# Moving the short convolution's elementwise work to VectorE and pacing the convolution units by weights

## The chip, the cores and the metric

One core of a Trainium2 chip runs the kernel. The metric is device time in microseconds (us) of one execution; smaller is better. The engines are TensorE (PE, with its weight loads shown as PEld), VectorE (DVE), ScalarE (ACT), GpSimd (POOL) and SyncE, whose queue (SPq) issues most transfers.

## The reference, cut to what matters

Two branches read the same layer-normed tokens (2048 tokens, 512 channels) and are added to the input.

```python
# branch A: short convolution of k, product with v, long convolution, gate
for t in range(4):
    k_shift += k_pad[:, t:t + S, :] * shift_k[:, 3 - t]
kv = k_shift * v
y  = irfft(rfft(pad(kv)) * rfft(pad(ssm_k)))[:S] + kv * ssm_D
A  = xn * y
# branch B: 8 experts, 2 for each token, gates by softmax over the two logits
h   = silu(xn @ w1[e]) @ w2[e]            # w1: 512 x 1792, w2: 1792 x 512
out = x + A + sum over e of gate * h
```

## The kernel before, in words

The experts are the spine of the program. They run one after the other (`expert`, rank 0 to 7, by falling number of tokens). For each, the weights come in slices: seven of w1 (128x1024 elements) and eight of w2 (128x896), seven of 128x1024 for the last three experts. ScalarE rounds a slice to float32r (`wh`, line 844), VectorE subtracts to get the rest (`wl`, line 847), and TensorE multiplies with high and low parts (line 862). In the first half each 128 hidden rows go from PSUM through Silu on ScalarE (`ht`, line 886) and two VectorE operations (`h`, lines 889 and 890). The next expert's tokens are gathered by an indirect transfer on the POOL queue (line 787), transposed on TensorE (`ptx`, line 806) and split by ScalarE and VectorE (`xh`, `xl`, lines 809 and 810). At an expert's end its outputs are gated and added (line 912) and scattered.

After every slice the expert calls `fill`, so there are 15 calls for each of the first five experts and 14 for the next two. `fill` hands out the other branch's work piece by piece. The list `units` has, in this order: two K units (`conv_k`, the last quarter of the long filter), eight V units (`conv_v`: two halves of the channels by four groups of tokens), two empty places, the exchange of the buffer pool (`swap`), 32 group units (`group_unit`, the middle stage of the transforms), and two empty places. Each call adds `rate` to a counter; when it has reached 1, the next unit is started and every unit under way is moved on by one stage. The rate is set so that the list is used up near call 87, near the end of the sixth expert. After that the 16 `last_unit`s follow in the last two experts, at 1.4 for each call of a first half.

A V unit has three stages. The first loads k and v (and, at the head of each half of the channels, the short filter's weights `shr`, line 683, copied to `sb` on VectorE, line 685) and does eight elementwise operations: `kva = k*w3` (line 712), three times `kvb = k*wt` and `kva += kvb` (lines 714, 715), `kva *= v` (line 716). Two of the four token columns are done by VectorE and two by GpSimd, each in 128x512 operations. The second stage splits `kva` into `vp` (ScalarE line 604, VectorE line 606), the third multiplies on TensorE (lines 610, 611) and stores to `zv_d`. The tiles of a V unit share seven buffers (tag b4), k has two.

A group unit loads `z` from `zk_d` and `zv_d`, splits it (lines 587, 590), multiplies (nine 512-column matmuls in all), and works on the products with ScalarE and VectorE (line 745 is its first VectorE operation after the matmuls) before the result is stored to `zi_d`.

The order of the instructions on each engine is fixed at build time: a planner simulates the program and lays each engine's instructions down by program order and by when it believes their inputs and buffers to be ready. Each engine then works its list strictly in order.

Of the kernel before, what the change touches and what calls it, by code (L numbers as in the profile page):

```python
# [18 lines left out]
P = 128  # L19
S = 2048  # L20
D = 512
DC = D // P
DH = D // 2
# [19 lines left out]
WARM = 4  # L43
DELAY = 3.0
STEPS = 8
RND = 1.5 * 2.0 ** 23
# [15 lines left out]
def fft_constants():  # L62
    """Matrices of the two-stage transform of odd frequencies kappa = k1 + 256 k2 of length 8192.

    Tokens are n = 32 n1 + n2.  The filter comes with runs of 16 on the partitions (2 n1 + n2 / 16), the
    other operand with the float32r parts of its data on one half of the partitions each (high and low,
    or low and high), and the matrices of the 64-point stages come to match.
    """
    n1 = np.arange(N1)
    k1 = 2 * np.arange(N1) + 1  # L70
    ang = 2 * np.pi * np.outer(n1, k1) / 256.0
    fwd = np.empty((N1, N1, 2))
    fwd[:, :, 0] = np.cos(ang)
    fwd[:, :, 1] = -np.sin(ang)
    fh, fl = _split(fwd.reshape(N1, P))
    inv = np.empty((N1, 2, N1))
    inv[:, 0, :] = np.cos(ang.T) * (2.0 / 4096.0)
    inv[:, 1, :] = -np.sin(ang.T) * (2.0 / 4096.0)
    ih, il = _split(inv.reshape(P, N1))
    zf, zi = np.zeros_like(fl), np.zeros_like(il)  # L80
    first = np.zeros((N1, 2, 2, 2, P), np.float32)
    for h in range(2):
        first[:, h, 0, h], first[:, h, 1, h] = fh, fl
    edge = np.concatenate([first.reshape(P, 4 * P), np.concatenate([fh, fh]), np.concatenate([fl, zf]),
                           np.concatenate([zf, fl]), il, ih, il, zi, ih, zi], axis=1)

    n2 = np.arange(N2)
    k2 = np.arange(N2)
    mid = np.empty((G, P, 4, P), np.float32)
    for g in range(G):  # L90
        b = np.zeros((2, 2, N2, 2, 2, N2))
        for a in range(2):
            kk = k1[2 * g + a]
            th = 2 * np.pi * (n2[:, None] * kk / 8192.0 + n2[:, None] * k2[None, :] / 32.0)
            b[a, 0, :, 0, a, :] = np.cos(th)
            b[a, 1, :, 0, a, :] = np.sin(th)
            b[a, 0, :, 1, a, :] = -np.sin(th)
            b[a, 1, :, 1, a, :] = np.cos(th)
        b = b.reshape(P, P)
        mid[g, :, 0], mid[g, :, 1] = _split(b)  # L100
        mid[g, :, 2], mid[g, :, 3] = _split(b.T)
    mid = mid.reshape(G // 2, 2, P, 4 * P).transpose(0, 2, 1, 3)
    return np.ascontiguousarray(edge), np.ascontiguousarray(mid).reshape(G // 2, P, 8 * P)
# [5 lines left out]
def routing_constants():  # L109
    """Index tables for the routing, the same for any input."""  # L110
    p = np.arange(P)
# [31 lines left out]
class Builder:  # L143
# [13 lines left out]

    # ------------------------------------------------------------------ setup
    def setup(self):
# [23 lines left out]
    def after(self, late, early, reason):  # L183
        """Keeps the program order of two instructions (no semaphore)."""
        self.tc.add_manual_dep(
            late.ins, early.ins.name,
            mybir.DependencyInfo(mybir.DependencyClass.NoSync, mybir.DependencyReason.DATA), reason=reason)

    # ------------------------------------------------- layer norm and routing
    def load_x(self, ep, sp, cp):  # L190
# [32 lines left out]
    def logits(self, bp, sp, cp):  # L223
        """The gate's logits before the scaling by rstd, x @ (w - mean(w)), and layer norm's statistics."""
        nc, io = self.nc, self.io
# [75 lines left out]
    def norm(self):  # L301
        """Normalises tokens in place; the last of them release the stores."""
        nc = self.nc
# [19 lines left out]
    def floor_div(self, out, x, tmp, d, scale):  # L323
        """out = scale * floor(x / d) for integers 0 <= x < 4096, by rounding x / d - (d - 1) / 2d."""
        V = self.nc.vector
# [4 lines left out]
    def routing(self, bp, sp, cp):  # L330
# [160 lines left out]
        def pick(dst, mask, a):  # L491
            """dst = a where mask else dst (a is lost)"""
            V.tensor_sub(a, a, dst)
            V.tensor_mul(a, a, mask)
            V.tensor_add(dst, dst, a)
# [23 lines left out]
    def onehot(self, A, q, parts):  # L519
        """A[:, i, :] = onehot(q[:, i])"""  # L520
        n, width = A.shape[1:]
# [12 lines left out]
    def products(self, A, B, R, srcs, out):  # L534
        """out = onehot(row)^T @ [onehot(column) * v for v in srcs]"""
        nc = self.nc
# [15 lines left out]
    def slots(self, cp):  # L552
        """Token and gate of every slot, a few of the tokens' columns at a time."""
        V = self.nc.vector
# [24 lines left out]

    # ------------------------------------------------------------- long conv  # L580
    def split_pair(self, pool, tag, src, shape, hi_eng="act", bufs=None):
        """src (float32 AP) -> float32r parts hi, lo with hi + lo = src."""
        nc = self.nc
# [15 lines left out]
    def split_halves(self, pair, src):  # L599
        """float32r parts of src: of its rows 0..63 high over low, of its rows 64..127 low over high."""  # L600
        nc = self.nc
# [6 lines left out]
    def edge1(self, out, h, pair):  # L608
        """First stage of the transform of one half's tokens."""
        self.nc.tensor.matmul(out, self.ev[:, 0, :], pair[h], start=True, stop=False)  # L610
        self.nc.tensor.matmul(out, self.ev[:, 1 + h, :], pair[h], start=False, stop=True)

    def tokens(self, ap):
        """[S, d] rows as [half, n1, n2 in the half, d]"""
        return ap.rearrange("(n h j) d -> h n j d", h=2, j=NI)
# [13 lines left out]
    def load_k(self, cp, dc):  # L629
        """Long filter of 128 channels, the skip weight added to its first tap."""  # L630
        nc, io = self.nc, self.io
# [10 lines left out]
    def conv_k(self, cp, dc, c8, routed):  # L642
        """First stage of the long filter's transform, 128 channels and every other run of 8 tokens."""
        nc = self.nc
# [32 lines left out]
    def conv_v(self, cp, dh, c4):  # L677
        """kv = shift_conv(k) * v and the first stage of its transform."""
        nc, io = self.nc, self.io
# [25 lines left out]
        b = cp.tile([P, 4, DH], F32, tag="b4", name="kvb")  # L705
        for eng, i0, i1 in ((nc.vector, 0, 2), (nc.gpsimd, 2, 4)):
            r = slice(i0, i1)

            def w(t):
                return sb[:, t:t + 1, :].to_broadcast([P, i1 - i0, DH])  # L710

            eng.tensor_mul(a[:, r, :], k[:, i0:i1, :], w(3))
            for t in (2, 1, 0):
                eng.tensor_mul(b[:, r, :], k[:, i0 + 3 - t:i1 + 3 - t, :], w(t))  # L714
                eng.tensor_add(a[:, r, :], a[:, r, :], b[:, r, :])  # L715
            eng.tensor_mul(a[:, r, :], a[:, r, :], v[:, r, :])
        yield
# [39 lines left out]
    def last_unit(self, gp, i):  # L757
        """Last stage for tokens i of every run of 16; the products with the matrix's low part come apart."""
        nc, io = self.nc, self.io
# [18 lines left out]

    # ------------------------------------------------------------------- moe
    def gathers(self, r):  # L780
# [36 lines left out]
    def prep(self, r):  # L817
        """Rank 0's tokens come as they are and are normalised here, the others' come from xn."""
        nc = self.nc
# [45 lines left out]
    def expert(self, hp, r, fill):  # L865
        """The expert with the r-th largest number of tokens, on its first CAPS[r] slots."""
        nc, io = self.nc, self.io
# [112 lines left out]
    def overflow(self):  # L980
        """Tokens beyond an expert's static slots, in blocks of 96; as many blocks as the routing asks for."""
        nc, io, tc = self.nc, self.io, self.tc
# [40 lines left out]
    def build(self):  # L1023
# [14 lines left out]
        with ExitStack() as st:  # L1038
# [13 lines left out]
            slots = self.slots(cp)  # L1052
            units = [lambda c8=c8: self.conv_k(cp, 3, c8, True) for c8 in range(2)]
            units += [lambda dh=dh, c4=c4: self.conv_v(cp, dh, c4) for dh in range(2) for c4 in range(4)]
            units += [None, None, swap]
            units += [lambda g=g: self.group_unit(self.gp, g) for g in range(G)]
            units += [None, None]
            lasts = [lambda i=i: self.last_unit(self.gp, i) for i in range(NI)] + [None]
            live = []
            done = [-DELAY]  # L1060
            rate = (len(units) + DELAY) / (5.75 * 15)

# [11 lines left out]
            def fill(r, second):  # L1074
                next(slots, None)
                if units:
                    done[0] += rate
                    while done[0] >= 1.0:
                        done[0] -= 1.0
                        step(units)  # L1080
                elif not second:
# [33 lines left out]
```

## Time and profile before

| | |
|---|---|
| median of 3 runs | 1073.06 us (1069.16 to 1077.16) |
| profiled execution, span from first to last instruction | 1070.0 us |
| PE busy | 886.5 us (83%) |
| DVE busy | 697.2 us (65%) |
| ACT busy | 471.5 us (44%) |
| POOL busy | 365.2 us (34%) |

The profiled execution is given by its span alone. Busy times are sums over the whole span, and the stages differ much: the page's line of 40 slices (26.75 us each) has TensorE at 9 tenths in slices 15 to 29, but at 3 to 9 tenths in slices 7 to 14, which is where the V units run, and at 3 to 8 in the last ten, where the last units run.

### The profile page before, as it was taken

The numbers are of one execution on the slowest core, as the hardware profiler recorded it, in microseconds if no ns is written. First come the engines' busy times: TensorE is split into PE (matmuls) and PEld (weight loads), VectorE is DVE, ScalarE is ACT, GpSimd is POOL, SyncE is SP. The second block draws the span as 40 slices with busy tenths as digits, with TensorE's granted clock in tenths as the row PEclk, the third lists the DMA queues.
The fourth block names the chain that finished last, engine by engine and source line by source line (L and its number), as shares of the span: only waits on it lengthen the run. The fifth ranks groups of instructions, "written<-read, shape, count | busy, mean of one in ns | idle before, by whom it ended". The sixth has DMA issues, their size and how long they took to land.

```text
span 1070.0 us, 14726 instructions
## 1 busy us (share of the span) xinstructions
PE 886.5 (83%) x5440; PEld 793.4 (74%) x5440; DVE 697.2 (65%) x986; ACT 471.5 (44%) x705; POOL 365.2 (34%) x279
## 2 busy tenths in 40 slices
PE   9879993986678899999999999999956786452595
PEld 7669993985667799999999999888744564341484
DVE  7879736999898786687668865895544530442431
ACT  5663231344233466666665765675423320322220
POOL 1362046894778422041204140500222113231213
PEclk9879997997988999999999999999987898685798
DMA  7788477866665865666566666664744445424332
GB/s 269 242 280 280 165 153 183 232 184 144 167 163 146 269 190 176 201 201 190 176 201 203 200 169 199 201 202 128 226 107 117 95 100 122 121 62 117 90 99 83
DMA packets 175526, 183.27 MB, mean 171 GB/s; under 512 B 38150, under 2 KB 138880, under 8 KB 173980
## 3 DMA queue, kind: packets, MB, share of 16 engines
q1 hardware_dynamic: 132556, 143.03, 44.9%
q0 software_dynamic: 42896, 39.27, 15.1%
q8 instruction: 44, 0.72, 0.3%
q14 instruction: 30, 0.25, 0.1%
HBM read 140.09 MB, written 46.45 MB: 174 GB/s over the span
## 4 chain that ended last, share of the span: by engine, by line
PE 43%; DMA 27%; DVE 10%; issue 9%; POOL 2%; ACT 1%; SPq 1%; ACTq 0%; POOLq 0%; DVEq 0%
PE ps L862 33%; DMA out_dram<-xnb 12%; DMA xnb<-xn_d 5%; DMA shr<-in_A_shift_k_dram 3%; DMA acc<-out_dram,gix 3%; DMA out_dram<-acc,ids 2%; DVE wl L847 2%; DVE kvb L714 2%; DVE kva L715 1%; DVE vp L606 1%; DMA zv_d<-ev 1%; PE ptx L806 1%; DMA zb<-zi_d 1%; DVE h L889 1%; POOL out_dram L914 1%
## 5 line engine op out<-in xcount | busy, mean ns | idle before, releaser
L847 DVE TENSOR_TENSOR wl<-wraw,wh 128x1024 fp32r<-128x1024 f32 (+1 forms) x112 | 140.3, 1253 | 119.2 <-ACT wh L844 110.4
L862 PE MATMUL ps<-xh,wh 128*128 128x264 f32 (+6 forms) x728 | 189.6, 322 | 32.4 <-DVE acc L912 20.7
L844 ACT ACTIVATE wh<-wraw 128x1024 fp32r<-128x1024 f32 (+1 forms) x117 | 119.5, 1022 | 192.6 <-PE ps L862 95.7
L862 PE MATMUL ps<-h,wh 128*128 128x264 f32 (+3 forms) x1120 | 193.5, 291 | 0.0
L862 PE MATMUL ps<-xl,wh 128*128 128x264 f32 (+6 forms) x728 | 186.9, 318 | 0.0
L862 PE MATMUL ps<-xh,wl 128*128 128x264 f32 (+6 forms) x728 | 185.9, 317 | 0.0
L862 PEld LDWEIGHTS ps<-h,wh 128*128 128x128 f32 x1120 | 162.9, 191 | 2.2
L862 PEld LDWEIGHTS ps<-xh,wh 128*128 128x128 f32 x728 | 124.3, 194 | 45.0 <-ACT yb L774 20.5
L862 PEld LDWEIGHTS ps<-xl,wh 128*128 128x128 f32 x728 | 123.3, 193 | 7.4
L862 PEld LDWEIGHTS ps<-xh,wl 128*128 128x128 f32 x728 | 122.8, 193 | 7.9
L862 PE MATMUL ps<-h,wl 128*128 128x264 f32 (+3 forms) x560 | 119.4, 292 | 1.8 <-DVE wl L847 1.8
L886 ACT ACTIVATE ht<-ps 128x528 f32<-128x528 f32 (+6 forms) x112 | 68.0, 607 | 72.4 <-PE ps L862 34.4
L914 POOL DMA_INDIRECT out_dram<-acc,ids x42 | 59.6, 1419 | 113.3 <-DVE acc L912 104.0
L862 PEld LDWEIGHTS ps<-h,wl 128*128 128x128 f32 x560 | 90.4, 192 | 3.1 <-DVE wl L847 2.1
L890 DVE TENSOR_TENSOR h<-ht,h 128x528 fp32r<-128x528 f32 (+6 forms) x112 | 89.1, 798 | 2.1
L590 DVE TENSOR_TENSOR lo<-zb,hi 128x1024 fp32r<-128x1024 f32 x16 | 19.6, 1222 | 103.4 <-ACT hi L587 102.8
L899 POOL DMA_INDIRECT acc<-out_dram,gix x42 | 56.4, 1342 | 86.0 <-issue 38.9
L771 PE MATMUL psb<-hi,ei 128*128 128x512 f32 x32 | 13.3, 496 | 71.0 <-ACT hi L587 71.0
L787 POOL DMA_INDIRECT xg<-xn_d,gix x36 | 46.2, 1282 | 74.7 <-DVE tb L548 41.0
L933 PE MATMUL py<-wh,h 128*128 128x512 f32 (+2 forms) x168 | 68.4, 408 | 3.9 <-ACT wh L844 3.9
L776 POOL TENSOR_TENSOR xnb<-xnb,yb 128x512 f32<-128x512 f32 x16 | 22.7, 1422 | 140.7 <-DMA xnb<-xn_d 134.2
L934 PE MATMUL py<-wl,h 128*128 128x512 f32 (+2 forms) x168 | 68.5, 408 | 0.6 <-DVE wl L847 0.6
(257 smaller groups left out, 1601.3 us busy)
## 6 DMA issues: line engine op xcount, KB each, us to landing
wraw<-in_B_w_dram SPq DMA_DIRECT2D x77, 512.0 KB
wraw<-in_B_w_dram SPq DMA_DIRECT2D x40, 448.0 KB
zk_d<-ev SPq DMA_DIRECT2D x16, 512.0 KB
zv_d<-ev SPq DMA_DIRECT2D x16, 512.0 KB
z<-zk_d SPq DMA_DIRECT2D x32, 256.0 KB
mid<-in_c_mid_dram POOLq DMA_DIRECT2D x16, 512.0 KB
z<-zv_d SPq DMA_DIRECT2D x32, 256.0 KB
zi_d<-zo SPq DMA_DIRECT2D x32, 256.0 KB
```

The lines of the kernel that those rows point to most:

```text
L714: eng.tensor_mul(b[:, r, :], k[:, i0 + 3 - t:i1 + 3 - t, :], w(t))
L776: nc.gpsimd.tensor_mul(xn, xn, y)
L787: self.gather = nc.gpsimd.indirect_dma_start(out=t[:sb], out_offset=None, in_=self.xn_d[:, :] if r else self.io["A_q"].rearrange("o s d -> ...
L844: w = nc.scalar.activation(hi, raw, AF.Copy)
L847: t = (lo_eng or nc.vector).tensor_sub(lo, raw, hi)
L862: nc.tensor.matmul(ps[:, u, :n], w, x[:, u, :], start=first and w is wh and k == 0, stop=last and w is wl)
L886: acts.append(nc.scalar.activation(t, ps[:, :nu, :n], AF.Silu))
L890: self.hid = nc.vector.tensor_sub(l, t, h)
L899: nc.gpsimd.indirect_dma_start(out=acc[:sb], out_offset=None, in_=io["out"][:, :], in_offset=bass.IndirectOffsetOnAxis(ap=self.gix[:sb, c0 ...
L914: st = nc.gpsimd.indirect_dma_start(out=io["out"][:, :], out_offset=bass.IndirectOffsetOnAxis(ap=self.ids[:sb, c0 + b:c0 + b + 1], axis=0) ...
L933: nc.tensor.matmul(o, a, wh[:, f, :], start=ff == 0, stop=False)
L934: nc.tensor.matmul(o, a, wl[:, f, :], start=False, stop=False)
```

## The change

Comments and docstrings are removed. In `conv_v` the loop over two engines goes: VectorE does all four token columns in eight 128x1024 operations for each unit, and GpSimd does none. In `build` each unit has a cost (1 for K units, for the empty places behind the V units and for `swap`, 2.5 for V units, 1 for group units and the last two places); `rate` is formed from the sum of the costs, and `fill` starts a unit when the counter has reached that unit's cost.

```diff
+COST_K, COST_V, COST_G = 1.0, 2.5, 1.0
...
-        for eng, i0, i1 in ((nc.vector, 0, 2), (nc.gpsimd, 2, 4)):
-            r = slice(i0, i1)
-
-            def w(t):
-                return sb[:, t:t + 1, :].to_broadcast([P, i1 - i0, DH])
-
-            eng.tensor_mul(a[:, r, :], k[:, i0:i1, :], w(3))
-            for t in (2, 1, 0):
-                eng.tensor_mul(b[:, r, :], k[:, i0 + 3 - t:i1 + 3 - t, :], w(t))
-                eng.tensor_add(a[:, r, :], a[:, r, :], b[:, r, :])
-            eng.tensor_mul(a[:, r, :], a[:, r, :], v[:, r, :])
+
+        def w(t):
+            return sb[:, t:t + 1, :].to_broadcast([P, 4, DH])
+
+        nc.vector.tensor_mul(a, k[:, 0:4, :], w(3))
+        for t in (2, 1, 0):
+            nc.vector.tensor_mul(b, k[:, 3 - t:7 - t, :], w(t))
+            nc.vector.tensor_add(a, a, b)
+        nc.vector.tensor_mul(a, a, v)
...
-            units = [lambda c8=c8: self.conv_k(cp, 3, c8, True) for c8 in range(2)]
-            units += [lambda dh=dh, c4=c4: self.conv_v(cp, dh, c4) for dh in range(2) for c4 in range(4)]
-            units += [None, None, swap]
-            units += [lambda g=g: self.group_unit(self.gp, g) for g in range(G)]
-            units += [None, None]
+            units = [(COST_K, lambda c8=c8: self.conv_k(cp, 3, c8, True)) for c8 in range(2)]
+            units += [(COST_V, lambda dh=dh, c4=c4: self.conv_v(cp, dh, c4)) for dh in range(2) for c4 in range(4)]
+            units += [(COST_K, None), (COST_K, None), (COST_K, swap)]
+            units += [(COST_G, lambda g=g: self.group_unit(self.gp, g)) for g in range(G)]
+            units += [(COST_G, None), (COST_G, None)]
...
-            rate = (len(units) + DELAY) / (5.75 * 15)
+            rate = (sum(c for c, _ in units) + DELAY) / (5.75 * 15)
...
-                    while done[0] >= 1.0:
-                        done[0] -= 1.0
-                        step(units)
+                    while units and done[0] >= units[0][0]:
+                        cost, u = units.pop(0)
+                        done[0] -= cost
+                        step([u])
```

## Rows read from the trace of the kernel before

**Rows 1.** Windows: stretch, its length, busy us (and count) by engine, PEclk, DMA share, GB/s.
```profile
170.00:372.00 202.00, 147.81 (x1016) 140.34 (x1015) 182.80 (x166) 71.61 (x103) 149.40 (x99) 0.87 0.69 181
372.00:750.00 378.00, 377.26 (x2591) 352.13 (x2592) 280.67 (x392) 240.80 (x365) 85.40 (x74) 1.00 0.62 189
...
362.00:372.00 10.00, 5.74 (x47) 5.52 (x45) 3.60 (x5) 1.06 (x2) 8.17 (x8) 1.00 0.94 283
```

**Rows 2.** Whom TensorE waited for from 170 to 372: us in total, times, longest.
```profile
PE ps L610 <- DVE vp L606: 20.6, 4, 10.1
PE ptx L806 <- DVE xl L810: 20.5, 2, 16.5
```

**Rows 3.** The chain that ended last: start, us, piece.
```profile
150.12 18.39 DMA shr<-in_A_shift_k_dram
...
827.33 13.76 DMA out_dram<-xnb
```

**Rows 4.** VectorE by form from 168 to 362: count, busy us, mean ns, idle before.
```profile
L714 DVE TENSOR_TENSOR kvb<-k,sb 128x512 f32<-128x512 f32 x24 | 30.1, 1252 | 0.2
L715 DVE TENSOR_TENSOR kva<-kva,kvb 128x512 f32<-128x512 f32 x24 | 27.3, 1137 | 0.5
L606 DVE TENSOR_TENSOR vp<-kva,vp 64x1024 fp32r<-64x1024 f32 x16 | 26.2, 1640 | 1.3 <-ACT vp L604 0.8
L890 DVE TENSOR_TENSOR h<-ht,h 128x552 fp32r<-128x552 f32 x14 | 18.3, 1305 | 0.2
L847 DVE TENSOR_TENSOR wl<-wraw,wh 128x1024 fp32r<-128x1024 f32 x12 | 18.2, 1515 | 2.0 <-PE ps L862 1.6 <-ACT wh L844 0.3
L847 DVE TENSOR_TENSOR wl<-wraw,wh 128x896 fp32r<-128x896 f32 x9 | 15.0, 1672 | 0.1
...
L712 DVE TENSOR_TENSOR kva<-k,sb 128x512 f32<-128x512 f32 x8 | 12.5, 1558 | 4.0 <-DMA zv_d<-ev 4.0
L716 DVE TENSOR_TENSOR kva<-kva,v 128x512 f32<-128x512 f32 x8 | 8.4, 1044 | 0.2
L912 DVE SCALAR_TENSOR_TENSOR acc<-pty,gate,acc 96x512 f32<-96x512 f32 x6 | 4.1, 736 | 0.0
...
L810 DVE TENSOR_TENSOR xl<-ptx,xh 128x276 fp32r<-128x276 f32 x8 | 3.1, 434 | 0.0
```

**Rows 5.** The same view from 450 to 700, where no V unit runs.
```profile
L847 DVE TENSOR_TENSOR wl<-wraw,wh 128x1024 fp32r<-128x1024 f32 x19 | 23.2, 1222 | 12.6 <-ACT wh L844 10.9 <-issue 1.6
L890 DVE TENSOR_TENSOR h<-ht,h 128x528 fp32r<-128x528 f32 x28 | 19.7, 706 | 0.5
L847 DVE TENSOR_TENSOR wl<-wraw,wh 128x896 fp32r<-128x896 f32 x16 | 17.5, 1092 | 9.1 <-ACT wh L844 8.9
...
L889 DVE CAST h<-ht 128x528 fp32r<-128x528 f32 x28 | 12.2, 437 | 1.2 <-ACT ht L886 1.2
```

**Rows 6.** Tile kvb: ns min/median/max, first and last start.
```profile
L714 DVE TENSOR_TENSOR kvb<-k,sb x24: 675/1632/1789, 170.3 to 347.8; 128x512 f32<-128x512 f32 x24
L714 POOL TENSOR_TENSOR kvb<-k,sb x24: 1256/1628/2247, 171.4 to 340.5; 128x512 f32<-128x512 f32 x24
```

**Rows 7.** Timeline of VectorE: start, us, operation, idle before and what ended it.
```profile
168.53 1.09 DVE L685 COPY sb<-shr 128x1024 f32<-128x1024 f32 x1 [15.81 <-DMA shr<-in_A_shift_k_dram]
```

**Rows 8.** Timeline of TensorE inside expert 1, first and last of 26 rows.
```profile
206.76 0.41 PE L862 MATMUL ps<-xl,wh 128*128 128x276 f32 x2
...
213.14 0.42 PE L862 MATMUL ps<-xh,wl 128*128 128x276 f32 x2
```

**Rows 9.** The first window of Rows 1 again, line 862's matmuls and weight loads alone.
```profile
170.00:372.00 202.00, 124.06 (x868) 118.93 (x867) 0.87 0.69 181
```

**Rows 10.** Line 745 (one for each group unit): as Rows 6; then two of its starts.
```profile
L745 DVE TENSOR_TENSOR ka<-pu,ka x32: 683/692/693, 378.4 to 741.7; 128x512 f32<-128x512 f32 x32
...
454.03 0.69 DVE L745 TENSOR_TENSOR ka<-pu,ka 128x512 f32<-128x512 f32 x1
463.83 0.69 DVE L745 TENSOR_TENSOR ka<-pu,ka 128x512 f32<-128x512 f32 x1 [2.39 <-ACT ka L741]
```

## The prediction

> **What bounds the kernel now.** I read the windows first. From 372 to 750 us TensorE is busy 377 of 378 us at a granted clock of 1.00; from 170 to 372 it is busy 148 of 202 us at 0.87, while VectorE is busy 183 us there, its highest share of any long stretch [rows 1]. That is the stretch of the V units. Next, who is waited for: TensorE's two largest waits there, 41 us together, are both for VectorE, for `vp` and for the next expert's `xl` [rows 2]. So VectorE sets the pace from 170 to 372, and TensorE from then to about 750. Behind that, the chain that ended last runs mostly through the last units' accumulating stores, 14 us and more each, one after the other [rows 3]; they begin at fixed places of experts 6 and 7, so the tail starts earlier by whatever the front gains and keeps its length.
>
> Why is VectorE full? By form, every one of its operations that reads two SBUF tiles is slow between 168 and 362: `wl` 1515 and 1672 ns, `h` 1305 [rows 4], against 1222, 1092 and 706 ns where no V unit runs [rows 5]. The reader is to see in `kvb` that a 128x512 operation takes 675 ns at best and 1632 in the median, which is GpSimd's own median of 1628 [rows 6]: the two engines go in step.
>
> **How much TensorE loses.** Inside expert 1, 50 matmuls of 276 columns take 213.14 - 206.76 = 6.38 us, 0.1276 each [rows 8]. The 1016 matmuls from 170 to 372 [rows 1] are 868 of line 862 [rows 9], 64 of the V units (512 columns, by columns 0.237 each) and 84 transposes (128 columns at most, 0.06). At full pace that is 110.8 + 15.2 + 5 = 131 us, so 71 of the 202 us are lost, as idle time and as matmuls at half clock after a wait.
>
> **The elementwise work.** Removed: 64 GpSimd operations, 1.63 us each in the median. They leave only the stretch's slowdown with them. Added on VectorE: 8 units x 8 operations of 128x1024, which read two SBUF tiles as `wl` does: 64 x 1.222 [rows 5] = 78.2 us. Removed there: lines 712, 714, 715, 716, which sum to 78.3 us [rows 4]. So VectorE does GpSimd's half for nothing. The rest gets cheaper: `vp` 26.2 to 16 x 1.222 = 19.6, `h` 18.3 to 14 x 0.73 (706 ns by columns) = 10.3, `wl` 18.2 + 15.0 to 14.7 + 9.8; with the casts, some 30 us. Whether the repeated operand `sb` costs more in a longer operation no row shows; its 512-column form at 675 ns bounds two halves at 1.35, so between 0 and 32 x 0.13 = 4 us more; I take 0, from the nearest row.
>
> Here a rule is to be weighed. By rows 4 and 6 the half on GpSimd buys VectorE no time. The Trainium skill, Perfetto Trace Analysis, "Optimizing Scalar/DVE Operations", says that work of a saturated VectorE may be offloaded, even to GpSimd, though it adds that the two share an SBUF read port and that it might not help. By its first half the sum comes out slower, rival C; by its second, as mine.
>
> **The pacing.** Counting the calls of `fill` (rate 50/86.25 = 0.580 before, 62/86.25 = 0.719 after): K units start at calls 6 and 7, not 7 and 9; V units at 11, 14, 18, 21, 25, 28, 32, 35, not 11, 13, 14, 16, 18, 19, 21, 23; the last V matmuls at 38, not 26; groups from 41 to 84, not 30 to 83; the list ends at call 87 in both, and the last units keep their calls. So the V work is spread over 28 calls, not 16.
>
> What those 28 calls cost each engine. TensorE: 672 x 0.1276 / 15 = 5.72 us a call, 160, plus 15 for V and 5 for transposes: 180 us. VectorE, for each expert: 7 x 1.222 + 8 x 1.092 + 14 x (0.437 + 0.706) [rows 5] + 3.1 + 4.1 [rows 4] = 40.5 us, 2.7 a call, 76 in 28 calls; V adds 78.2 + 19.6 + 2 copies of `sb` (1.1 each): 176 us in all. The two are even, so VectorE's idle share decides. Bounds for its busy share: 0.905 (182.80 of 202) and 0.74 (280.67 of 378) [rows 1]. It is nearest to the first, a stretch with the same V chain: 176/0.905 = 194 us, 14 more than TensorE needs; the other end gives 238.
>
> The loads and stores of the V units (on SP's queue, four to six loads and two stores each) move with them, V7's by 12 calls, behind as many slices' weight loads; the bytes are the same and the stretch's DMA share of 0.69 [rows 1] falls, so I cost them at nothing; the cover is the three buffers of weights. POOL's queue loses what stood ahead of its gathers: also 0. K's transposes and matmuls move one or two calls up inside expert 0, where TensorE is busy anyway: 0.
>
> The stall at 150: `sb` waits 15.81 us for `shr` [rows 7], issued at 150.12 and 18.4 us under way [rows 3]. It takes a buffer that K0's parts held; K0 is done two calls (11 us) earlier after the change, so the load can be. Between 0 and the whole 15.8 us of VectorE stays; TensorE's wait for `xl` behind it was 16.5 [rows 2]. I take that it fits into the 14 above; if all stays, about 10 more.
>
> The group units: 32 in 43 calls, not 53. Nothing is added, but VectorE's load there rises by a tenth or so; the price lies between 0 and rival B's. I take 3 us. The wait for the first `z`, about 4 us idle at 362 to 372 [rows 1], stays.
>
> **Sum.** 71 - 4 - 14 - 3 = 50 us. The profiled execution, known by its span of 1070.0, becomes 1020; the runs' median of 1073.06 stands 3 above that span, so 1023.
>
> **Rivals.**
> A, smaller gain: VectorE, in order and near full, waits more for ScalarE's `wh` and `ht`, as it does later in the kernel (10.9 and 8.9 us before `wl` [rows 5]). At a busy share of 0.82, the middle of the bounds, the V stretch takes 215 us, 21 more: 1044; at 0.74, 238 us: 1067. That the planner does not follow the weights and starts V units as early as buffers allow ends here too, as bursts.
> B, slower: the group units' own chain (load, ScalarE, VectorE, TensorE, back) sets their pitch. Before, line 745 runs from 378.4 to 741.7, 11.7 us a unit [rows 10]. V stretch and empty places take 194 + 2 x 6 = 206 us after, against 19 calls or 19 x 5.72 + 20 + 67 = 196 before; with the old pitch kept, nothing is caught up: 1073 + 10 = 1083, and a little more makes 1090. It decides from a pitch of 11.6 on; TensorE alone would ask for 10.1 (7.3 us a call x 1.39). Against it: two neighbours at 454.03 and 463.83 [rows 10] are 9.8 us apart, with TensorE full.
> C, slower, by the rule above: VectorE's own time for its half is 64 x 0.69 = 44 us, so the change adds 34 to a full engine: 1107. Its page: the Trainium skill, Perfetto Trace Analysis. Against it stand the 78.3 us measured.
>
> **How the numbers follow.** Forecast 0.64 (1006, with nearly all lost time back, to 1035), A 0.22 (of it 0.04 within 1%), B 0.11 (0.05 within 1%, 0.06 beyond), C 0.03. About 1%, 10.7 us, is what a measurement here can tell from no change. Faster 0.64 + 0.18 = 0.82, same 0.09, slower 0.09. The range 1006 to 1058 holds the forecast and A without its upper end, and leaves out less than 0.2.
>
> **What would show it.** Elementwise rows of 1.22 us x 64 on VectorE, none on GpSimd; `wl` at 1.22 and 1.09 throughout; TensorE's waits for `vp` and `xl` below 15 us in all; the first group near 365 to 380 us; their pitch near 10; the tail as long as before. Wrong if the `kvb` rows exceed 1.4 us, if VectorE's idle share between the first and last V unit passes 15%, or if line 745 keeps 11.7 us.

## The result, and the profile after

The changed kernel takes 1041.45 us (median of 4 runs, 1038.40 to 1046.81); the kernel before, beside it, 1073.19 (4 runs, 1069.16 to 1077.16). The ratio is 0.9705, with a 95% interval of 0.9679 to 0.9732: faster by 32 us. Forecast were 1023 us and a range of 1006 to 1058: the sign and the range hold, but the gain is 32 us where the sum had 50. The profiled execution has a span of 1039.1 us, 30.9 shorter.

First the windows that answer to [rows 1]; the second row reaches from the first V unit's first operation to the last V unit's last matmul:

```profile
170.00:372.00 202.00, 194.41 (x1472) 190.44 (x1471) 160.91 (x191) 87.41 (x132) 62.91 (x46) 0.98 0.87 210
153.00:358.00 205.00, 197.41 (x1493) 193.51 (x1492) 171.90 (x204) 89.96 (x139) 71.70 (x51) 0.98 0.88 207
372.00:750.00 378.00, 370.13 (x2343) 334.84 (x2344) 282.67 (x391) 242.00 (x361) 79.94 (x68) 0.99 0.62 190
```

From 170 to 372 TensorE now does 1472 matmuls, not 1016, and is idle for 7.6 us, not 54, at a granted clock of 0.98, not 0.87. The bound of the front has changed hands: TensorE is nearly full, and VectorE fell from 183 to 161 us of the same 202, although it does GpSimd's half as well.

VectorE by form from 168 to 362, the view of [rows 4] (count, busy us, mean ns, idle before):

```profile
L714 DVE TENSOR_TENSOR kva<-kva,kvb 128x1024 f32<-128x1024 f32 x21 | 25.6, 1221 | 0.1
L713 DVE TENSOR_TENSOR kvb<-k,sb 128x1024 f32<-128x1024 f32 x21 | 25.6, 1218 | 9.9 <-DMA zv_d<-ev 9.8
L607 DVE TENSOR_TENSOR vp<-kva,vp 64x1024 fp32r<-64x1024 f32 x16 | 19.5, 1220 | 2.5 <-ACT vp L605 2.1
L846 DVE TENSOR_TENSOR wl<-wraw,wh 128x1024 fp32r<-128x1024 f32 x13 | 15.8, 1218 | 1.3 <-ACT wh L843 1.3
L846 DVE TENSOR_TENSOR wl<-wraw,wh 128x896 fp32r<-128x896 f32 x14 | 15.2, 1087 | 10.7 <-ACT wh L843 10.7
L889 DVE TENSOR_TENSOR h<-ht,h 128x552 fp32r<-128x552 f32 x14 | 10.2, 730 | 0.0
```

All that reads two SBUF tiles is back at the durations that [rows 5] show without V units: `wl` at 1218 and 1087 ns, not 1515 and 1672. The new operations cost 1.22 us each, and a repeated operand `sb` costs nothing on top. The tile `kvb` (ns minimum, median and maximum, first and last start) has one row, VectorE's, where [rows 6] has two:

```profile
L713 DVE TENSOR_TENSOR kvb<-k,sb x24: 1210/1218/1226, 155.4 to 341.5; 128x1024 f32<-128x1024 f32 x24
```

TensorE's waits from 170 to 372, all that are over 1 us (us in total, times, longest); the two of [rows 2], 41 us, are gone:

```profile
PE pty L976 <- DVE acc L911: 3.8, 1, 3.8
PE ptx L805 <- ACT ev L627: 2.0, 1, 2.0
PE ps L861 <- ACT ht L885: 1.8, 2, 1.1
```

VectorE's first copy of `shr` [rows 7] stands behind the operation before it and no longer behind a transfer:

```profile
153.08 1.09 DVE L686 COPY sb<-shr 128x1024 f32<-128x1024 f32 x1
```

So far the front went much as forecast. Where the rest of the gain went is seen from four tiles' rows: the group units' first VectorE operation [rows 10], their last result stored to `zi_d`, the combining of the outputs of experts 5 to 7, and the last units' accumulating stores. Of after:

```profile
L744 DVE TENSOR_TENSOR ka<-pu,ka x32: 676/692/694, 373.9 to 713.0; 128x512 f32<-128x512 f32 x32
L754 SPq DMA_DIRECT2D zi_d<-zo x32: 319/320/432, 386.6 to 725.0; - x32
L911 DVE SCALAR_TENSOR_TENSOR acc<-py,gate,acc x12: 736/750/752, 706.2 to 1028.0; 128x512 f32<-128x512 f32 x4, 127x512 f32<-127x512 f32 x4, 126x512 f32<-126x512 f32 x4
L776 POOL DMA_DIRECT2D out_dram<-xnb x16: 1350/1359/1543, 746.6 to 1005.2; - x16
```

The last three of before:

```profile
L755 SPq DMA_DIRECT2D zi_d<-zo x32: 319/320/503, 392.4 to 753.2; - x32
L912 DVE SCALAR_TENSOR_TENSOR acc<-py,gate,acc x12: 742/750/751, 763.7 to 1058.9; 128x512 f32<-128x512 f32 x4, 127x512 f32<-127x512 f32 x4, 126x512 f32<-126x512 f32 x4
L777 POOL DMA_DIRECT2D out_dram<-xnb x16: 1353/1362/1530, 775.7 to 1036.1; - x16
```

Expert 5's combining comes 57.5 us earlier (763.7 to 706.2), but the last store to `zi_d` only 28.2, and the first accumulating store only 29.1. From that store to the end it is 294.3 us before (1070.0 - 775.7) and 292.5 after. The gain is therefore 29.1 of an earlier start and 1.8 of a shorter tail. What the first accumulating store waits for has changed too; GpSimd's timeline (start, us, operation, idle before and what ended it), before and then after:

```profile
775.67 1.53 POOL L777 DMA_DIRECT2D out_dram<-xnb  x1 [4.04 <-DMA out_dram<-acc,ids]
```

```profile
746.59 1.54 POOL L776 DMA_DIRECT2D out_dram<-xnb  x1 [0.31 <-POOL xnb L775]
```

Before, its own data had been ready for 4 us and it waited for the scatter of expert 5's output. After, that scatter is long done, and it waits for its data: for the end of the group units. The two inputs of the tail, expert 5's output and the groups' results, are two streams of work, and the later one starts it. The chain of after that ended last (start, us, piece) shows the way:

```profile
725.01 5.63 DMA zi_d<-zo
730.70 3.94 DMA zb<-zi_d
...
746.59 15.79 DMA out_dram<-xnb
762.45 10.97 DMA xnb<-xn_d
...
775.66 14.65 DMA out_dram<-xnb
790.38 8.82 DMA xnb<-xn_d
```

From there on, each store of a last unit frees the `xnb` buffer for a later unit's load: 16 and 15 us for the stores, 11 and 9 us for the loads, one after the other.

### The profile page after: what moved, and what is told of

The parts are those of the page before. It is cut to its first block, busy times and chain, and to the rows that moved or that the text cites. A ratio compares the mean times of both kernels' runs of the same rounds, so it can differ in the third digit from the quotient of the medians.

```text
span 1039.1 us, 14657 instructions
## 1 busy us (share of the span) xinstructions
PE 876.3 (84%) x5440; PEld 788.0 (76%) x5440; DVE 667.7 (64%) x986; ACT 470.0 (45%) x705; POOL 269.7 (26%) x215
## 4 chain that ended last, share of the span: by engine, by line
PE 53%; DMA 29%; issue 4%; POOL 3%; DVE 3%; ACT 2%; POOLq 0%; another core or an unknown queue 0%; DVEq 0%; ACTq 0%; SPq 0%
PE ps L861 39%; DMA out_dram<-xnb 12%; DMA xnb<-xn_d 6%; DMA mid<-in_c_mid_dram 2%; DMA acc<-out_dram,gix 2%; DMA out_dram<-acc,ids 2%; DMA zv_d<-ev 2%; PE py L933 1%; PE py L932 1%; PE py L934 1%; POOL xg L786 1%; PE ptx L805 1%; PE pty L976 1%; POOL xnb L775 1%; POOL acc L898 1%
## 5 line engine op out<-in xcount | busy, mean ns | idle before, releaser
L846 DVE TENSOR_TENSOR wl<-wraw,wh 128x1024 fp32r<-128x1024 f32 (+1 forms) x112 | 131.5, 1174 | 110.6 <-ACT wh L843 103.8
L861 PEld LDWEIGHTS ps<-h,wh 128*128 128x128 f32 x1120 | 160.5, 188 | 1.7
L913 POOL DMA_INDIRECT out_dram<-acc,ids x42 | 63.7, 1516 | 159.6 <-DVE acc L911 146.4
L889 DVE TENSOR_TENSOR h<-ht,h 128x528 fp32r<-128x528 f32 (+6 forms) x112 | 81.2, 727 | 1.9
L786 POOL DMA_INDIRECT xg<-xn_d,gix x36 | 53.9, 1498 | 76.3 <-DMA wraw<-in_B_w_dram 47.9
L588 ACT ACTIVATE hi<-zb 128x1024 fp32r<-128x1024 f32 x16 | 16.9, 1055 | 124.6 <-DMA zb<-zi_d 124.6
```

The source lines that it names most:

```text
L588: nc.scalar.activation(hi, src, AF.Copy)
L786: self.gather = nc.gpsimd.indirect_dma_start(out=t[:sb], out_offset=None, in_=self.xn_d[:, :] if r else self.io["A_q"].rearrange("o s d -> ...
L846: t = (lo_eng or nc.vector).tensor_sub(lo, raw, hi)
L861: nc.tensor.matmul(ps[:, u, :n], w, x[:, u, :], start=first and w is wh and k == 0, stop=last and w is wl)
L889: self.hid = nc.vector.tensor_sub(l, t, h)
L913: st = nc.gpsimd.indirect_dma_start(out=io["out"][:, :], out_offset=bass.IndirectOffsetOnAxis(ap=self.ids[:sb, c0 + b:c0 + b + 1], axis=0) ...
```

## The experiments

Ratios are to the kernel before, run beside each on the same chip; times inside a kernel are of its profiled execution.

**The elementwise work without the weights.**

```diff
-COST_K, COST_V, COST_G = 1.0, 2.5, 1.0
+COST_K, COST_V, COST_G = 1.0, 1.0, 1.0
```

> The engine move alone: all elementwise work of the V units on VectorE, every unit at weight 1, so V units at the calls of the kernel before (11 to 23). Theory (the end of the group units sets the end; TensorE's gain in front of it counts only as far as it moves them): VectorE gets 100 us of V work in 16 calls, not 28, so TensorE waits some 30 us again between 170 and 350, but the groups start nearer to the front of the program; last group's store near 715 to 735 us, total 1035 to 1055, the contention removed being most of the gain. Rival (the weights carry the gain, the engine move only feeds them): total 1060 or more, as before.

1040.76 us, ratio 0.9660 [0.9601, 0.9719]: as fast as the whole change. The last `zi_d` store starts at 705.4, earlier than expected (715 to 735), and the first accumulating store at 730.5. TensorE idles 14.4 us from 170 to 350 (165.61 of 180 busy), where some 30 were expected. Without the weights the `shr` wait is back, and TensorE's wait for `xl` behind it (timelines of VectorE and TensorE):

```profile
169.06 1.12 DVE L686 COPY sb<-shr 128x1024 f32<-128x1024 f32 x1 [16.39 <-DMA shr<-in_A_shift_k_dram]
```

```profile
179.90 2.10 PE L805 MATMUL ptx<-ident,xg 92*128 92x92 f32 x12 [8.11 <-DVE xl L809]
```

So the weights remove that stall, but what they give at the front they take from the groups, which start 21 us later with them (373.9, not 352.4). The first accumulating store is 16.1 us earlier than in the changed kernel, but from there to the end it is 303.5 us, not 292.5, so the profiled execution is only 5.1 us shorter: an early first store alone does not shorten the kernel by as much.

**The weights without the elementwise work**: the changed kernel with the two-engine loop of before.

```diff
-        nc.vector.tensor_mul(a, k[:, 0:4, :], w(3))
...
+        for eng, i0, i1 in ((nc.vector, 0, 2), (nc.gpsimd, 2, 4)):
...
```

> The weights alone: V units at weight 2.5 as in the changed kernel, but the elementwise work shared by VectorE and GpSimd as before. Theory: operations of both engines stay slow (kvb 1.6 us for 512 columns, wl 1.5 or more), VectorE needs some 206 us for the stretch in which TensorE needs 180, so the first group comes near 385 to 400 us, 15 to 30 later than with the whole change; total 1055 to 1075. Rival (spreading is what pays): total within 8 us of the changed kernel's 1041.

1087.89 us, ratio 1.0101 [1.0036, 1.0166]: slower than expected. The tile `kvb` on both engines, then `wl` by form from 168 to 380:

```profile
L716 DVE TENSOR_TENSOR kvb<-k,sb x24: 671/692/3584, 159.2 to 378.2; 128x512 f32<-128x512 f32 x24
L716 POOL TENSOR_TENSOR kvb<-k,sb x24: 1252/1619/2264, 164.9 to 369.7; 128x512 f32<-128x512 f32 x24
```

```profile
L849 DVE TENSOR_TENSOR wl<-wraw,wh 128x1024 fp32r<-128x1024 f32 x14 | 23.3, 1666 | 1.4 <-ACT wh L846 1.4
```

`wl` is still slow beside GpSimd's operations, at 1666 ns, not 1218, now over a longer stretch. VectorE's `kvb` was expected at 1.6 us; its median is 0.69 here and its longest 3.58, so other operations than before pay for the overlap. The first group's line comes at 415.9 (385 to 400 expected), the last `zi_d` store at 769.9. Within this change the gain is the elementwise work's alone.

**Five buffers for the last units' loads** (tag "ka", which the group units' products use as well).

```diff
-        a = gp.tile([P, D], F32, tag="ka", name="ka", bufs=2)
+        a = gp.tile([P, D], F32, tag="ka", name="ka", bufs=5)
...
-        xn = gp.tile([P, D], F32, tag="ka", name="xnb", bufs=2)
+        xn = gp.tile([P, D], F32, tag="ka", name="xnb", bufs=5)
```

> The changed kernel with five buffers, not two, for the tile that a last unit loads, multiplies and stores with accumulation (and that a group unit uses for its products). Theory: the tail is a chain of store, load into the freed buffer, multiply, store; with five buffers the load no longer waits for a store, so the 111 us from the first to the ninth accumulating store shrink to 60 to 80 and the total falls to 985 to 1015. Rival (the accumulating stores are slow in themselves or TensorE's last two experts set the tail): total 1035 to 1045.

1021.57 us, ratio 0.9488 [0.9427, 0.9548]. From the first accumulating store (761.7) to the end it is 256 us, not 292: the buffers do limit the tail. The first nine stores start within 88 us, not 111; 60 to 80 were expected. But the store starts 15 us later than in the changed kernel, so the total misses the expected 985 to 1015. SP's queue and ScalarE show why:

```profile
708.87 9.88 SPq L764 DMA_DIRECT2D xnb<-xn_d  x4
718.95 11.04 SPq L836 DMA_DIRECT2D wraw<-in_B_w_dram  x2
730.09 3.15 SPq L754 DMA_DIRECT2D zi_d<-zo  x1
```

```profile
740.43 0.60 ACT L753 ACTIVATE zo<-pz 128x512 f32<-128x512 f32 x1 [15.09 <-DMA zi_d<-zo]
```

The early loads and the weights' loads hold the queue for 21 us, the last `zi_d` stores stand behind them, and ScalarE waits 15 us for the one `zo` buffer to come free.

**The youngest unit first.** In the changed kernel the units under way are moved on oldest first, so one group's last three matmuls (`pz`) stand on TensorE right ahead of the next group's first (`pk`). TensorE and VectorE of after, two groups:

```profile
489.22 0.39 PE L596 MATMUL pz<-hi,mid 128*128 128x512 f32 x1
489.45 0.39 PE L596 MATMUL pk<-hi,mid 128*128 128x512 f32 x1
...
498.83 0.40 PE L596 MATMUL pz<-hi,mid 128*128 128x512 f32 x1
499.06 0.40 PE L596 MATMUL pk<-hi,mid 128*128 128x512 f32 x1
```

```profile
491.57 0.69 DVE L744 TENSOR_TENSOR ka<-pu,ka 128x512 f32<-128x512 f32 x1
...
496.80 0.69 DVE L591 TENSOR_TENSOR lo<-ka,hi 128x512 fp32r<-128x512 f32 x1 [0.76 <-ACT hi L588]
```

`pz` at 498.83 needs `lo`, made at 496.80 at the end of a chain from `pk` and `pu` at 489.45 over ScalarE and VectorE; the next group's `pk`, whose inputs were ready, stands behind that `pz`. So the chain of one group sets the earliest start of the next, although TensorE hardly idles (370 of 378 us busy): it works on expert matmuls, and the experts run ahead of the groups. The kernel before has the same order:

```profile
461.48 0.40 PE L595 MATMUL pz<-hi,mid 128*128 128x512 f32 x1
461.71 0.40 PE L595 MATMUL pk<-hi,mid 128*128 128x512 f32 x1
```

The second line starts the group whose VectorE row stands at 463.83 in [rows 10]. The 9.8 us between those two neighbours are thus the chain's own pitch, as the 9.6 above are.

```diff
-                for u in list(live):
+                for u in list(live)[::-1]:
```

> The changed kernel with one edit: when a unit starts, the units under way are moved on youngest first, so a group's first products no longer stand behind the last product of the group before it, which waits for that group's whole chain on ScalarE and VectorE. Theory: the groups' pitch of 10.9 us is this chain; it falls to 10.0 to 10.5, the last group's store comes at 695 to 712 us, not 725, and the total falls by as much, to 1012 to 1030. Rival (something else, the loads or TensorE, sets the pitch, or the tail is set by experts 6 and 7): pitch 10.8 or more, or an earlier last group with a total of 1036 to 1046.

1032.03 us, ratio 0.9587 [0.9523, 0.9652]; 2 us above the expected total. Two rows of tiles:

```profile
L744 DVE TENSOR_TENSOR ka<-pu,ka x32: 676/691/693, 369.5 to 695.5; 128x512 f32<-128x512 f32 x32
...
L754 SPq DMA_DIRECT2D zi_d<-zo x32: 319/320/368, 382.0 to 706.8; - x32
```

The pitch (the mean time from one group to the next) falls from (713.0 - 373.9)/31 = 10.94 to (695.5 - 369.5)/31 = 10.52 us, the last store to `zi_d` comes at 706.8, where 695 to 712 was expected, and the first accumulating store at 728.1. The order of the units was a part of the lost gain.

**The changed kernel again**, unaltered, as the yardstick for a second set of kernels.

> The changed kernel unaltered, to stand on the same chip beside the others of this batch. Both theories: 1036 to 1046.

1047.22 us, 1 above the expected, ratio 0.9722 [0.9683, 0.9762]; last `zi_d` store 730.9, expert 5's combining 712.1, first accumulating store 752.5: the groups' end again decides.

**Half of VectorE's elementwise work left out**, all weights 1.

```diff
-        nc.vector.tensor_mul(a, k[:, 0:4, :], w(3))
+        r = slice(0, 2)
+        nc.gpsimd.memset(a[:, 2:4, :], 1.0)
+        nc.vector.tensor_mul(a[:, r, :], k[:, 0:2, :], w(3))
...
```

> VectorE alone, units at weight 1, but half of the V units' elementwise work left out: VectorE does its two token columns in 128x512 operations as before, GpSimd only fills the other two with a constant (so the long convolution's input is wrong in half of its tokens). Theory (contention slowed VectorE; VectorE's second half of the work is then nearly free): kvb at 0.69 us, TensorE idle under 15 us from 170 to 372, last group's store 690 to 705 us, total 1005 to 1030, at most 30 below the engine move alone. Rival (the V units' own chain of loads, buffers and stages holds TensorE up, not contention): TensorE idle over 30 us there and total 1040 or more.

1036.31 us, ratio 0.9641 [0.9589, 0.9692]: both expectations missed. TensorE idles 24.5 us of 202 (177.47 busy), which neither theory had. `kvb` takes 685 ns in the median, as alone in [rows 6], so the engine has room, but both halves of the channels wait for `shr`:

```profile
167.34 1.09 DVE L686 COPY sb<-shr 128x1024 f32<-128x1024 f32 x1 [15.96 <-DMA shr<-in_A_shift_k_dram]
...
242.05 1.07 DVE L686 COPY sb<-shr 128x1024 f32<-128x1024 f32 x1 [13.80 <-DMA shr<-in_A_shift_k_dram]
```

Half of the work gone buys 4 us against the first experiment, within the intervals. Once GpSimd is out, VectorE's elementwise load is not what the time hangs on, here with all weights 1; with the changed kernel's weights it was not run.

**All three together**: youngest first, four buffers for tag "ka", and two for `zo`, meant to take away the stall of the buffer experiment.

```diff
-        zo = gp.tile([P, D], F32, tag="zo", name="zo")
+        zo = gp.tile([P, D], F32, tag="zo", name="zo", bufs=2)
```

> The changed kernel with youngest first, four buffers for the last units' tile and two for the group units' output, whose store a blocked queue had held up when the first was tried with five. Theory (the groups' end and then the chain of accumulating stores set the end): last group's store 700 to 712 us, from there to the end some 280 instead of 316; total 980 to 1000. Rival (TensorE's work in experts 6 and 7 or the accumulating stores themselves set the tail once the groups end earlier): total 1010 to 1030.

999.44 us, ratio 0.9282 [0.9246, 0.9318], the fastest version here.

```profile
L776 POOL DMA_DIRECT2D out_dram<-xnb x16: 1347/1357/1537, 747.5 to 958.1; - x16
```

The first accumulating store is no earlier than in the changed kernel; the tail is 255 us long (1002.6 - 747.5). The last `zi_d` store, at 718.9, missed the expected 700 to 712, and the first accumulating store follows it by 28.6 us, not 21.6. SP's queue shows why:

```profile
711.44 7.39 SPq L836 DMA_DIRECT2D wraw<-in_B_w_dram  x1
718.92 3.71 SPq L754 DMA_DIRECT2D zi_d<-zo  x1
730.76 1.22 SPq L760 DMA_DIRECT2D zb<-zi_d  x2
```

The last `zo` was made at 712.1, but its store stands behind a load of weights and starts 6.8 us later; `zb` is then loaded 11.8 us after the store's start, where it is 5.7 in the changed kernel. The second `zo` buffer spares ScalarE its wait, but the queue still holds the store up.

**The same with all weights 1.**

```diff
-COST_K, COST_V, COST_G = 1.0, 2.5, 1.0
+COST_K, COST_V, COST_G = 1.0, 1.0, 1.0
```

> As the run before with every unit at weight 1 in place of 2.5 for V units. Theory (the weights bring nothing by themselves where the engine move is made): within 10 us of it. Rival (with the groups' chain relaxed TensorE in front of it counts, and spreading the V work pays): 10 to 30 us slower than it.

1015.17 us, ratio 0.9438 [0.9402, 0.9474]: the theory missed, its rival was right. The copy of `shr` waits 14.65 us, TensorE is busy 183.62 of 202 us from 170 to 372, expert 5 is combined at 738.9, not 713.8. So the weights are worth nothing in the changed kernel and 16 us here. Of the 9.0 us between the two profiled executions 2.7 lie before the first accumulating store (750.2, not 747.5) and the rest behind it. The last expert's last combining, first here, then with the weights, then in the changed kernel:

```profile
1004.55 0.75 DVE L911 SCALAR_TENSOR_TENSOR acc<-py,gate,acc 126x512 f32<-126x512 f32 x1 [2.03 <-PE py L934]
```

```profile
995.66 0.75 DVE L911 SCALAR_TENSOR_TENSOR acc<-py,gate,acc 126x512 f32<-126x512 f32 x1 [2.03 <-PE py L934]
```

```profile
1028.03 0.75 DVE L911 SCALAR_TENSOR_TENSOR acc<-py,gate,acc 126x512 f32<-126x512 f32 x1 [0.64 <-DMA acc<-out_dram,gix]
```

In the changed kernel it waits for a transfer that stands behind the accumulating stores; with more buffers it waits for TensorE, so the experts' earlier progress counts again.

**Two buffers for `zh` and `zl`** (one for `yh`, `yl` in exchange), against the idea that buffers hold the groups' pitch.

```diff
-        zh, zl = self.split_pair(gp, "z", z, [P, 2, D])
+        zh, zl = self.split_pair(gp, "z", z, [P, 2, D], bufs=2)
```

> The changed kernel with two buffers, not one, for the split parts of a group unit's input (and one, not two, for those of its products, to make room). Theory (a group's first products stand on TensorE behind the last product of the group before, which waits for that group's chain): nothing moves, pitch 10.8 to 11.1, last group's store 720 to 733, total 1036 to 1050. Rival (the split has to wait until the group before has left its buffers): last group's store before 712, total below 1032.

1049.12 us, ratio 0.9706 [0.9668, 0.9743]; pitch (720.5 - 381.2)/31 = 10.95 us. Nothing changes, so more buffers for the split parts alone are not what is missing. One buffer of `yh`, `yl` was given up for them, so a gain that this took back is not ruled out; against it, in the changed kernel the split parts for the `pk` at 499.06 are ready at 495.4.

**The kernel before, youngest first.**

```diff
-                for u in list(live):
+                for u in list(live)[::-1]:
```

> The kernel before with the one edit youngest first. Theory (the first accumulating store comes 12 us after expert 5's combining or 22 after the last group's store, whichever is later; in the kernel before both give 775): the groups end earlier, but expert 5 does not, so the first accumulating store stays within 8 us of 775 and the total within 10 of the kernel before. Rival (the groups' end alone sets the tail): total 15 or more below the kernel before, as with the changed kernel.

1086.12 us, ratio 1.0074 [1.0035, 1.0113]. The order that gave the changed kernel some 10 us gives the kernel before none. The total is within 10 us, as expected, but the way there is another: the groups were to end earlier and end later (last `zi_d` store at 765.7, not 753.2), because they start later (line 745 first at 395.7, not 378.4) while their pitch falls only to 11.54 us. Expert 5 is combined at 775.6, and the first accumulating store comes at 787.5, 12.5 later than 775, where at most 8 were expected. So this run does not show what earlier groups alone would be worth in the kernel before.

**One rule over nine kernels**, all that keep two `xnb` buffers. The first accumulating store starts about 12 us after expert 5's first combining or about 21.6 us after the last store to `zi_d`, whichever is later. Starts in us:

| kernel | combining + 12 | last `zi_d` store + 21.6 | first accumulating store |
|---|---|---|---|
| before | **775.7** | 774.8 | 775.7 |
| after | 718.2 | **746.6** | 746.6 |
| after, again | 724.1 | **752.5** | 752.5 |
| without the weights | **730.4** | 727.0 | 730.5 |
| weights alone | 763.0 | **791.5** | 791.9 |
| youngest first | 720.5 | **728.4** | 728.1 |
| half left out | **735.1** | 734.1 | 734.8 |
| before, youngest first | **787.6** | 787.3 | 787.5 |
| two `zh`, `zl` | 725.8 | **752.2** | 755.9 |

The two offsets were fitted to before and after; the other seven starts follow from them to 0.4 us, but for the last, 3.7. GpSimd's rows agree on which of the two decides: before this store the engine idles 3.2 to 4.3 us until the scatter of expert 5's output has landed in the four kernels whose first column is bold, and 0.31 us, with its own data the last to come, in the other five. The rule gives the tail's start only; its length is 292 to 298 us in eight of the nine, and 303.5 without the weights. In the kernel before the two were 0.9 us apart by this rule, and 4 us by GpSimd's row above. That is why a combining that came 57.5 us earlier gave 29.

## Why the prediction was right, and where it was too high

**The elementwise work: right.** 64 operations of 1.22 us replace operations that took the same time in the sum, and the rest of VectorE's work got cheaper, as the rows by form show. That the gain is this part's, and not the pacing's, is shown by 0.9660 for it alone and 1.0101 for the weights alone. The Trainium skill's suggestion (Perfetto Trace Analysis, "Optimizing Scalar/DVE Operations") that handing work of a saturated VectorE to GpSimd may make sense does not hold here; its remark that this might not help does. Rival C is out.

**The V stretch: the loss right, the reason not.** By the prediction's own prices the 1472 matmuls from 170 to 372 (1298 of line 861, 64 of the V units, 108 transposes, two of a group) need some 188 us at full pace, so 14 of the 202 are lost, as taken; 7.6 of them are idle time. But the stretch from the first V unit's first operation to the last V matmul took 205 us, not 194, and VectorE's idle share did not decide it. VectorE is busy 171.90/205 = 0.84 there, not 0.905, so it passes the 15% of idle time that was named as a sign of being wrong; TensorE is busy 197 us, where I had counted 180, and waits for VectorE 3.8 us in all. Rival A's waits came (12 us of VectorE before `wl`, for ScalarE's `wh`), but they cost TensorE next to nothing; that its 1044 us is near the result is chance.

**The `shr` stall: right.** The long one, at the first copy, is gone with the weights, and there in all three kernels with weights of 1 that were run. **The first `z`: wrong, in my favour.** TensorE is busy 26.00 of 26 us from 346 to 372:

```profile
346.00:372.00 26.00, 26.00 (x200) 25.41 (x199) 9.88 (x11) 10.26 (x15) 7.34 (x8) 1.00 0.79 243
```

**The group units: the step that failed.** "I take 3 us" rested on a pitch of 10.1 us that TensorE alone would ask for, and on two neighbours 9.8 apart [rows 10], which were read as room and were the units' own chain. Measured is 10.94, so 31 x 0.84 = 26 us. With the terms as measured the sum is 71 - 0 - 14 - 26 = 31, which is the 31 us by which the profiled execution is shorter; without the groups it is 57, which is what expert 5's end gained. The prices of the 14 are rough, so that it comes out to the microsecond is chance. It is rival B's mechanism at less than its price: the units' own chain does hold the pitch, above 10.1 and below the 11.6 from which that rival decides. That the order of the units carries a part of it is shown (10.52 with the youngest first); what holds the rest, 0.4 us a unit, is open.

**The tail: the assumption that let the step cost this much.** "The tail starts earlier by whatever the front gains" holds for expert 5's end (57.5 us earlier; the sum had 53 without the groups), but the last units need the groups' results as well, and these came 28 us earlier. "And keeps its length" was right: 294.3 and 292.5 us. The chain of waits in [rows 3] showed stores that free buffers; I read it as the tail's length and did not ask which of two inputs its first store had waited for, and how far behind the other one was. In the kernel before the answer was 4 us.

## What to carry to other kernels

Where a stage needs two streams of work, look at how long before the later one the earlier one was ready: beyond that slack a gain in one stream is worth only what the other gains too, and here the slack was 4 us at most, against a gain of 57. Read the pitch of a chain of units that follow one another on an in-order engine from the order in which their instructions stand, not from the engine's busy time: TensorE was busy 370 of 378 us, yet the units came late because other work filled the gaps. A step that is worth nothing in one kernel (the weights in the changed one) can be worth over 1% when the stage that took its gain back is relaxed, so try it again behind each removed bound.

## What the runs showed of the hardware

- VectorE and GpSimd on the same two-input f32 operation of 128x512 (`kvb`) in the kernel before: medians of 1.63 us on each, where VectorE takes 0.68 to 0.69 without the other and GpSimd 1.25 at its fastest. The Trainium skill (SBUF — State Buffer, "Who interferes with whom") says that VectorE operations with two SBUF inputs contend with GpSimd's reads of SBUF, and this slowdown agrees. One strictly after the other would take 0.69 + 1.25 = 1.94 us, more than the 1.63 of the median.
- An accumulating store of 256 KB from the GpSimd queue takes 14 to 20 us from issue to landing in the chain of after, and a load of 256 KB beside it 9 to 11 us.
- SP's queue passed a stall on: with five buffers, 21 us of load issues became a 15 us wait of ScalarE for a buffer whose store stood behind them.
